# Attention and bilinear feed-forward on one core: probability sums by accumulating transfers in place of GpSimd and half of VectorE's additions

## The chip, the cores and the metric

The kernel runs on one core of a Trainium2 chip. The metric is the device time of one execution in microseconds (us), the median of several runs. The engines of the core are named as in the profile: PE is TensorE's matmul, PEld its weight loads, DVE is VectorE, ACT is ScalarE, POOL is GpSimd, SP is SyncE. L585 is line 585 of the kernel.

## What is computed

Attention in which a query sees only the keys whose nearest centroid is the same as its own, and then a bilinear feed-forward layer on its output:

```python
batch, n_heads, seq, head_dim = (4, 8, 768, 64); n_clusters = 16
q_assign = np.argmax(einsum('bhsd,hcd->bhsc', q_n, c_n), -1)   # same for k
mask = q_assign[:, :, :, None] == k_assign[:, :, None, :]
scores = scale * np.matmul(q, k.transpose(0, 1, 3, 2))
scores = np.where(mask, scores, -1000000000.0)
scores = scores - np.max(scores, axis=-1, keepdims=True)
attn = np.exp(scores)
attn = attn / (np.sum(attn, axis=-1, keepdims=True) + 1e-09)
attn_out = np.matmul(attn, v)
# bridge: x is (4 * 768, 512), then with d_ff = 1536
a = x @ w_a
b = x @ w_b
out = a * b @ w_out
```

## The kernel before

Two heads are worked on at a time, a head pair `p`; there are 4 per batch element (`HP = 4`) and 16 in all. A pair has two halves of 384 queries (`HB = 384`), and each half six key tiles of 128 keys (`j` = 0 to 5). One half and one key tile make a unit `u`. Scores are laid out with keys on the partitions, so the sum over the keys, which the softmax divides by, has to be taken across partitions. The kernel first adds the six tiles of exponentials into one tile `acc` and then multiplies a matrix of ones by it.

The scores of two units are made, then their exponentials. There are four buffers for the exponentials `pt`, two for `acc` and two for the scores:

```python
ptp = pool("ptp", 4)
accp = pool("accp", 2)
...
ps_s = pool("ps_s", 2, PS)
...
        def exp():
            for u, s in zip(us, tiles):
                pt = ptp.tile([P, 2, HB], FP32, name="pt")
                nc.scalar.activation(out=pt, in_=s[:, :, 0:HB], func=AF.Exp,
                                     scale=SCALE)                      # L563
                probs[u] = pt
```

The additions, one instruction for each of the two heads `a`. In batch element 0 (`p < HP`) all are on VectorE and the sixth tile is left to the matmul with ones; in the others GpSimd takes most:

```python
    def add_up(u):
        p, hf, j = where(u)
        if j == 0 or j == NJ - 1 and p < HP:
            return
        if j == 1:
            accs[p, hf] = accp.tile([P, 2, HB], FP32, name="acc")
        acc = accs[p, hf]
        for a in range(2):

            many = p >= HP and (a == 1 or j > 3)
            eng = nc.gpsimd if many else nc.vector
            eng.tensor_tensor(                                         # L585
                out=acc[:, a, :],
                in0=probs[u - 1][:, a, :] if j == 1 else acc[:, a, :],
                in1=probs[u][:, a, :], op=ALU.add)
```

The sum across partitions, and the division. `across`, `invert` and `back` run on VectorE (L639, L642, L646), `apply` on GpSimd (L653) with one exception:

```python
    def denominators(p, hf):
        ps = apart()
        acc = accs.pop((p, hf))
        terms = [acc]
        if p < HP:
            terms.insert(0, probs[p * UPP + hf * NJ + NJ - 1])
        for n, t in enumerate(terms):
            for a in range(2):
                nc.tensor.matmul(out=ps[a * D:(a + 1) * D, 0:HB], lhsT=ones,
                                 rhs=t[:, a, :], start=(n == 0),        # L619
                                 stop=(n == len(terms) - 1))
        ...
    def normalize(p, hf):
        ...
        def apply():
            eng = nc.vector if (p, hf) == (HP - 1, 0) else nc.gpsimd
            eng.tensor_tensor(out=x, in0=x, in1=den, op=ALU.mult)       # L653
```

The loop over groups of two units. Each engine works through its own instructions in the order in which they stand here:

```python
    for g in range(NG + 3):
        p, l = divmod(g, GPP)                  # GPP = 6 groups per head pair
        now = (2 * g, 2 * g + 1)
        before = (2 * g - 2, 2 * g - 1)
        ...
        if 0 < g < NG:
            score(now)                         # TensorE, then the exponentials
        check_inverses()
        if 0 < g <= NG:
            for u in before:
                add_up(u)
        flush_w()
        if 1 < g <= NG:
            weigh(before)                      # probabilities by v, TensorE
        late = int(g > EARLY)                  # EARLY = 25
        if g % 3 == late and 0 < g - late:
            ... denominators(...)              # of the half that ended
        if g < NG:
            ready[l]()
        ...                                    # pieces of the feed-forward layer
        # (TensorE; PSUM read by ScalarE and VectorE), steps of normalize, and
        # the rounding of weight parts, are spread over the rest of the group
```

The feed-forward layer of one batch element runs between the groups of the next. GpSimd also multiplies in it (`done`, L824), and adds in the rounding of the 36 parts of the weights (`round_w`, L295); VectorE waits for that addition in `flush_w` (L302).

Of the kernel before, what the change touches and what calls it, by code (L numbers as in the profile page):

```python
# [14 lines left out]
ALU = mybir.AluOpType  # L15
# [123 lines left out]
def short_path(nc, tc, ctx, c, cn, centroids_in, casts, n_far, q, k, v,  # L139
# [7 lines left out]
    HP = H // 2  # L147
# [387 lines left out]
    probs, accs, O_of, den_of, xTs = {}, {}, {}, {}, {}  # L535
# [5 lines left out]
    def where(u):  # L541
        p, l = divmod(u, UPP)
        hf, j = divmod(l, NJ)
        return p, hf, j
# [29 lines left out]
# [4 lines that stand above are left out]
        if j == 1:  # L578
            accs[p, hf] = accp.tile([P, 2, HB], FP32, name="acc")
        acc = accs[p, hf]  # L580
        for a in range(2):

            many = p >= HP and (a == 1 or j > 3)
            eng = nc.gpsimd if many else nc.vector
            eng.tensor_tensor(  # L585
                out=acc[:, a, :],
                in0=probs[u - 1][:, a, :] if j == 1 else acc[:, a, :],
                in1=probs[u][:, a, :], op=ALU.add)

    def weigh(us):  # L590
        for u in us:
# [497 lines left out]
    for g in range(NG + 3):  # L1089
        p, l = divmod(g, GPP)  # L1090
# [9 lines left out]
# [3 lines that stand above are left out]
# [300 lines left out]
```

## Time and profile before

| | |
|---|---|
| time, median of 3 runs | 1044.93 us (1044.05 to 1045.06) |
| span of the profiled run | 1042.1 us |
| granted TensorE clock | 0.998 |
| transfers, all queues | 46.49 MB, 120523 packets |
| additions of exponentials, VectorE | 136 of 128 x 384 |
| additions of exponentials, GpSimd | 168 of 128 x 384 |

Times of instructions are given as a sum in us and a mean in ns, with the shape of the output and the inputs. Behind the bar stands the idle time of the engine just before them and the instruction that ended most of it. Matmuls overlap in TensorE, so a group's busy time is shorter than count times mean.

### The profile page before, as it was taken

What the parts mean: (1) busy time and instruction counts of PE and PEld (TensorE: products, weight loads), DVE (VectorE), ACT (ScalarE), POOL (GpSimd) and SP (SyncE); (2) the same over time, 40 slices, a digit from 0 to 9 for tenths busy, and PEclk for the clock granted to TensorE, in tenths of its full rate; (3) what the DMA queues carried; (4) which work ended last, traced back from release to release, by engine and by line L of the source; (5) the groups of instructions that cost most, each with busy time, mean ns of one, the idle gap of its engine ahead of it and who ended that gap; (6) DMA issues with size and microseconds to landing.
All of it is one profiled execution on the core that took longest, in us unless ns stands there. A gap on an engine that the chain in (4) does not pass through costs nothing.

```text
span 1042.1 us, 17904 instructions
## 1 busy us (share of the span) xinstructions
PE 1030.8 (99%) x7158; PEld 500.5 (48%) x7158; DVE 658.7 (63%) x1314; ACT 302.8 (29%) x590; POOL 334.1 (32%) x310
## 2 busy tenths in 40 slices
PE   8999999999999999999999999999999999999997
PEld 5443444444445554444444555444444565444565
DVE  6777888889847447555546746755454835554652
ACT  5665333233322222332323122333232201111100
POOL 1111255555633332343443421444333310211100
PEclk9999999999999999999999999999999999999999
DMA  7334253525220121203020030300000000000001
GB/s 183 87 86 86 70 123 105 127 70 142 63 49 21 30 51 27 35 4 47 5 46 4 23 66 25 46 2 20 1 5 1 12 30 22 1 1 1 3 30 34
DMA packets 120523, 46.49 MB, mean 45 GB/s; under 512 B 106608, under 2 KB 115824, under 8 KB 120432
## 3 DMA queue, kind: packets, MB, share of 16 engines
q1 hardware_dynamic: 120016, 44.85, 18.7%
q8 instruction: 58, 0.95, 0.4%
q10 hardware_dynamic: 416, 0.43, 0.1%
q14 instruction: 33, 0.27, 0.1%
HBM read 37.78 MB, written 6.29 MB: 42 GB/s over the span
## 4 chain that ended last, share of the span: by engine, by line
PE 95%; DVE 2%; issue 1%; POOL 0%; DMA 0%; ACT 0%; DVEq 0%; POOLq 0%
PE m L679 63%; PE s L554 15%; PE O L596 13%; PE s L619 2%; PE m L619 1%; PE s L370 1%; PE m L370 0%; PE m L354 0%; DMA h<-in_q_dram 0%; DVE xT L910 0%; DVE raw L910 0%; PE m L430 0%; POOL xT L653 0%; PE m L384 0%; DVE h L919 0%
## 5 line engine op out<-in xcount | busy, mean ns | idle before, releaser
L563 ACT ACTIVATE pt<-s 128x768 f32<-128x768 f32 x192 | 145.3, 809 | 202.5 <-PE s L554 146.4
L585 POOL TENSOR_TENSOR acc<-acc,pt 128x384 f32<-128x384 f32 x144 | 155.6, 1100 | 60.0 <-ACT pt L563 45.9
L596 PE MATMUL O<-pt,v 128*64 128x384 f32 x768 | 145.1, 499 | 0.0
L554 PE MATMUL s<-qkT 64*128 64x384 f32 x768 | 139.7, 483 | 0.0
L824 POOL TENSOR_TENSOR h<-h,ha 128x384 f32<-128x384 f32 x54 | 56.1, 1041 | 255.6 <-DVE ha L818 255.1
L679 PE MATMUL m<-xT,wb_sb 128*64 128x384 f32 x672 | 116.4, 487 | 0.0
L679 PE MATMUL m<-xT,wa_sb 128*64 128x384 f32 x672 | 116.2, 487 | 0.2 <-DVE xT L653 0.2
L818 DVE TENSOR_TENSOR ha<-ha,m 128x384 f32<-128x384 f32 x72 | 39.6, 551 | 106.5 <-PE m L679 80.4
L815 ACT COPY h<-m 128x384 f32<-128x384 f32 x72 | 34.4, 478 | 184.9 <-PE m L679 184.9
L596 PEld LDWEIGHTS O<-pt,v 128*64 128x64 f32 x768 | 46.7, 136 | 85.7 <-issue 80.0
L679 PE MATMUL m<-wo_sb,h 128*64 128x256 f32 x768 | 86.7, 380 | 0.0
L554 PEld LDWEIGHTS s<-qkT 64*128 64x128 f32 x768 | 70.7, 187 | 31.2 <-issue 0.2
L818 DVE TENSOR_TENSOR h<-h,m 128x384 f32<-128x384 f32 x72 | 39.5, 549 | 72.3 <-PE m L679 46.9
L679 PE MATMUL m<-raw 128*64 128x384 f32 x432 | 78.9, 486 | 0.0
L653 POOL TENSOR_TENSOR xT<-xT,acc 128x384 f32<-128x384 f32 x31 | 32.5, 1048 | 143.2 <-DVE acc L646 143.0
L679 PEld LDWEIGHTS m<-xT,wb_sb 128*64 128x64 f32 x672 | 47.9, 137 | 61.2 <-issue 56.3
L679 PEld LDWEIGHTS m<-xT,wa_sb 128*64 128x64 f32 x672 | 48.0, 137 | 60.4 <-issue 55.6
L679 PEld LDWEIGHTS m<-wo_sb,h 128*64 128x64 f32 x768 | 55.0, 137 | 31.0 <-issue 5.0
L585 DVE TENSOR_TENSOR acc<-acc,pt 128x384 f32<-128x384 f32 x96 | 63.4, 687 | 2.3 <-ACT pt L563 1.0
L679 PE MATMUL m<-xT,h 128*64 128x256 f32 x576 | 64.5, 379 | 0.0
L679 PE MATMUL m<-xT,size 128*64 128x384 f32 x288 | 52.7, 487 | 0.0
L679 PEld LDWEIGHTS m<-xT,h 128*64 128x64 f32 x576 | 41.4, 137 | 22.3 <-issue 2.0
(168 smaller groups left out, 1312.3 us busy)
## 6 DMA issues: line engine op xcount, KB each, us to landing
raw<-in_moe_w_a_dram SPq DMA_DIRECT2D x12, 512.0 KB, 3.9
raw<-in_moe_w_b_dram SPq DMA_DIRECT2D x12, 512.0 KB, 3.6
raw<-in_moe_w_out_dram SPq DMA_DIRECT2D x12, 512.0 KB, 3.7
qk<-in_q_dram SPq DMA_DIRECT2D x48, 96.0 KB, 3.2
qk<-in_k_dram SPq DMA_DIRECT2D x48, 96.0 KB, 3.6
v<-in_v_dram SPq DMA_DIRECT2D x24, 192.0 KB, 3.8
out_dram<-rest SPq DMA_DIRECT2D x24, 128.0 KB, 1.7
v<-in_v_dram SPq DMA_DIRECT2D x4, 384.0 KB, 4.5
```

The costliest lines, as they stand in the source:

```text
L370: nc.tensor.matmul(out=ps[32 * kq:32 * kq + 32, 0:HB], lhsT=cTb[:, hp, :], rhs=qkTs[p][:, kq * HB:(kq + 1) * HB], start=True, stop=True)
L554: nc.tensor.matmul(out=s[:, a, 0:HB], lhsT=Ts[p][r, S + j * P:S + (j + 1) * P], rhs=Ts[p][r, hf * HB:(hf + 1) * HB], start=start, stop=not ...
L563: nc.scalar.activation(out=pt, in_=s[:, :, 0:HB], func=AF.Exp, scale=SCALE)
L585: eng.tensor_tensor(out=acc[:, a, :], in0=probs[u - 1][:, a, :] if j == 1 else acc[:, a, :], in1=probs[u][:, a, :], op=ALU.add)
L596: nc.tensor.matmul(out=O_of[0][a * D:(a + 1) * D, 0:HB], lhsT=vs[p][:, a, j, :], rhs=probs[u][:, a, :], start=(j == 0), stop=(j == NJ - 1))
L619: nc.tensor.matmul(out=ps[a * D:(a + 1) * D, 0:HB], lhsT=ones, rhs=t[:, a, :], start=(n == 0), stop=(n == len(terms) - 1))
L653: eng.tensor_tensor(out=x, in0=x, in1=den, op=ALU.mult)
L679: nc.tensor.matmul(out=ps[half], lhsT=lhsT[:, half], rhs=rhs, **kw)
L815: nc.scalar.copy(out=box[name], in_=box["X"][:, 0:HB])
L818: nc.vector.tensor_tensor(out=box[name], in0=box[name], in1=box[bank][:, 0:HB], op=ALU.add)
L824: nc.gpsimd.tensor_tensor(out=to, in0=to, in1=box[name], op=ALU.mult)
```

## The change

The sums of batch element 0 stay on VectorE, but both heads are added in one instruction of 768 columns. In batch elements 1 to 3, VectorE adds the first two key tiles of a half in one instruction, and each of the four others is added by a transfer, issued by GpSimd, that reads the tile of exponentials and adds it to `acc` where it lies. The aim is to take the additions off VectorE and GpSimd, and to have them done by the DMA engines.

```diff
@@ def add_up(u):
         if j == 1:
             accs[p, hf] = accp.tile([P, 2, HB], FP32, name="acc")
         acc = accs[p, hf]
-        for a in range(2):
-
-            many = p >= HP and (a == 1 or j > 3)
-            eng = nc.gpsimd if many else nc.vector
-            eng.tensor_tensor(
-                out=acc[:, a, :],
-                in0=probs[u - 1][:, a, :] if j == 1 else acc[:, a, :],
-                in1=probs[u][:, a, :], op=ALU.add)
+        if p < HP:
+            nc.vector.tensor_tensor(out=acc, in0=probs[u - 1] if j == 1 else acc,
+                                    in1=probs[u], op=ALU.add)
+            return
+        if j == 1:
+            nc.vector.tensor_tensor(out=acc, in0=probs[u - 1], in1=probs[u],
+                                    op=ALU.add)
+        else:
+            nc.gpsimd.dma_start(out=acc, in_=probs[u], accum_op=ALU.add)
```

In the changed kernel the lines behind this place are one further on: L619 becomes L620, L653 becomes L654.

## The prediction

> **What bounds the kernel now.** I read the engine table of the page first, then the stretches of the span, then who TensorE waited for, then GpSimd's groups, and last the timeline around the end of one half of a head pair.
>
> From the page and from the table of stretches (time, then busy time of PE, PEld, DVE, ACT, POOL with counts, granted clock, DMA share, GB/s):
>
> ```profile
> PE 1030.8 (99%) x7158; PEld 500.5 (48%) x7158; DVE 658.7 (63%) x1314; ACT 302.8 (29%) x590; POOL 334.1 (32%) x310
> ...
> 0.00:104.00 104.00, 99.78 (x672) 47.99 (x672) 79.07 (x164) 61.59 (x110) 18.04 (x22) 1.00 0.46 111
> 104.00:208.00 104.00, 103.26 (x646) 44.33 (x648) 90.88 (x139) 36.46 (x67) 48.21 (x39) 1.00 0.42 106
> 208.00:312.00 104.00, 104.00 (x664) 45.49 (x662) 81.21 (x123) 35.74 (x69) 55.63 (x46) 1.00 0.34 81
> 312.00:840.00 528.00, 527.67 (x3700) 256.62 (x3698) 307.25 (x641) 145.47 (x290) 189.75 (x182) 1.00 0.12 24
> 840.00:1042.00 202.00, 196.09 (x1484) 106.06 (x1478) 100.33 (x251) 23.55 (x54) 22.49 (x23) 0.99 0.05 14
> ```
>
> TensorE is the bound, with no slack. The probability sums of batch elements 1 to 3 are made from 104 to 840 us, 736 us in which PE is busy for all but 1.07 us (0.74 + 0 + 0.33). Its other idle time is 4.2 us before 104 us and 5.9 us behind 840 us; behind 840 us next to no sums are made. Removing work from DVE or POOL can therefore give back next to nothing. From the groups by shape and the list of waits:
>
> ```profile
> L585 POOL TENSOR_TENSOR acc<-acc,pt 128x384 f32<-128x384 f32 x144 | 155.6, 1100 | 60.0 <-ACT pt L563 45.9 <-DVE acc L585 11.5
> L585 POOL TENSOR_TENSOR acc<-pt 128x384 f32<-128x384 f32 x24 | 29.6, 1232 | 0.9
> L585 DVE TENSOR_TENSOR acc<-acc,pt 128x384 f32<-128x384 f32 x96 | 63.4, 687 | 2.3 <-ACT pt L563 1.0
> L585 DVE TENSOR_TENSOR acc<-pt 128x384 f32<-128x384 f32 x40 | 24.9, 638 | 14.9 <-POOL xT L653 10.3 <-ACT pt L563 4.6
> ...
> PE m L619 <- DVE acc L585: 2.1, 1, 2.1
> ```
>
> The 304 additions cost 273.5 us of two engines that are not the bound. One matmul in the whole run waited for a sum: 2.1 us, in batch element 0. So the question is only whether the new transfers are late for TensorE. From the timeline of GpSimd and ScalarE:
>
> ```profile
> 636.61 1.37 POOL L585 TENSOR_TENSOR acc<-pt 128x384 f32<-128x384 f32 x1
> 638.06 2.48 POOL L585 TENSOR_TENSOR acc<-acc,pt 128x384 f32<-128x384 f32 x2
> 654.30 1.00 POOL L653 TENSOR_TENSOR xT<-xT,acc 128x384 f32<-128x384 f32 x1 [13.76 <-DVE acc L646]
> 655.25 4.08 POOL L585 TENSOR_TENSOR acc<-acc,pt 128x384 f32<-128x384 f32 x4
> ...
> 665.55 1.51 ACT L563 ACTIVATE pt<-s 128x768 f32<-128x768 f32 x2 [0.68 <-PE s L554]
> ```
>
> The last two key tiles (four additions of one head each) are summed from 655.25 to 659.33 us; the matmuls with ones that read the sum start at 667.33 us, 8 us later. GpSimd reached these additions only at 655.3, because the multiplication of L653 stands ahead in its queue and waited for DVE.
>
> **What the Trainium skill says.** (1) "DMA: Bandwidth & Descriptors", section "Anatomy of one DMA — SWDGE (gpsimd) path": a transfer issued by GpSimd costs about 2.0 us plus its bytes at 436 GB/s. No such transfer is in this trace; the nearest, 12 KB from SBUF to SBUF issued by SyncE (ohT<-oh), lands in 1.8 us. (2) "Collectives: The Full Stack", section "The bandwidth ceiling: the fold count and why AG ≠ RS ≠ AR": an adding transfer runs at half the rate of a copy, because of two source reads and not because of the addition. No run here shows it yet. (3) "DMA: Bandwidth & Descriptors", section "Rules for kernel authors": an accumulating transfer must await the earlier one to the same bytes. The built program agrees: each of a half's second to fourth transfers waits for the completion of the one before. (4) "SBUF — State Buffer", section "Who interferes with whom": a DVE instruction with two SBUF inputs contends with GpSimd's reads. The trace agrees: the DVE additions have a median of 552 ns and a maximum of 1632.
>
> **The change, part by part.**
>
> *Removed.* GpSimd loses 168 additions: 155.6 + 29.6 = 185 us of its 334. All lie beside TensorE's work: 0 us on the path.
>
> *VectorE in one instruction.* Batch element 0 has 8 halves of 4 additions, before 64 instructions of 384 columns, now 32 of 768. DVE takes 550 ns for 384 columns and 414 for 256 (L818, L942), so 1.06 ns a column, and 768 should take about 0.96 us instead of 2 x 0.55. Elements 1 to 3 keep one addition of 768 per half (24 of them) where 72 of 384 were. DVE's 136 additions (63.4 + 24.9 = 88.3 us) become 56 of 0.96, or 54 us: DVE falls from 659 to some 625. Worth on the path: part of the one 2.1 us wait; I put down 1 us.
>
> *Added.* 24 halves x 4 key tiles = 96 transfers, each 128 x 768 x 4 B = 393 KB from SBUF to SBUF, issued by GpSimd in its queue, four in a row dependent on each other. Their latency L, from issue to landing, is the number that decides. By the skill's formula with twice the data: 2.0 + 2 x 0.90 = 3.8 us. By the trace: packets of 1024 B have a median of 48 ns and of 4096 B of 159 ns (packet records), so 0.036 ns a byte and about 122 ns for a row of 3072 B; 128 rows over 16 engines, read twice, are 8 x 2 x 122 = 1.95 us; with 1.8 us of fixed time (ohT<-oh) and about 1 us for GpSimd to write the descriptors (my estimate, from the skill's remark that this path's first byte takes about 1 us), 4.8 us. I take 4.8, and think 3.8 to 7 likely.
>
> *What TensorE tolerates.* In the half shown, the transfer of tile 5 (the fifth) goes out at 655.3, that of tile 6 at 655.3 + L, and lands at 655.3 + 2L. The matmuls at 667.3 allow L of up to 6.0; the exponentials of 665.55 and 666.26, which reuse the two buffers the transfers read, allow 10.2 and, by 2L = 10.96, 5.5. A group of two key tiles takes 8.3 to 12 us of TensorE (distances between the exponentials), so in other halves the limit is lower. I laid such a chain through all 24 halves: exponentials, matmuls and GpSimd's other instructions where the trace has them, GpSimd held 1 us by each issue, no feedback. The sum of how late the sums come to their matmuls:
>
> - L = 4.0: 1.5 us in 2 halves; 4.5: 4.5 us in 4; 5.0: 13 us in 8
> - L = 5.5: 26 us in 11; 6.0: 44 us in 14; 7.0: 105 us in 23
>
> At 4.8 that is about 9 us. GpSimd also stands still while a transfer waits for the one before, and with it the multiplications of L653 and L824 and, until 36 weight parts are rounded, L295, for which DVE waits in L302 and so drains PSUM later. From 24 halves I add some 3 us. Sum: 1044.9 - 1 + 9 + 3 = 1056 us.
>
> **Rivals.** *Hidden anyway*: if L is 4.2 or less, every sum is there in time and the kernel ends at 1043 to 1047. For it: the formula's 3.8, and DMA engines only 12% busy from 312 to 840 us. Against: the 512 KB weight loads need 3.6 to 3.9 us with one read, and from 104 to 312 us the DMA engines are already 34 to 42% busy. *The transfers become the bound*: four dependent ones per half against about 30 us of TensorE (736 / 24 = 30.7). At L = 6.5 the list gives over 60 us, near 1115; at 8 (4 x 8 = 32) the chain is as long as the half itself and the time goes past 1150. For it: the addition's rate is shown nowhere in this trace. *GpSimd's blocked queue* is the third: with short transfers still, delayed L295 or L653 hold DVE, PSUM banks fill, and some 10 to 20 us are lost in the first two stretches. Against: GpSimd loses 185 us of work, and TensorE has three PSUM banks in turn. *A gain of over 2%* would need 21 us of PE's 11.3 us idle time; it can't come from this change.
>
> **Range and chances.** The 2% limit, 1065.8 us, is crossed at L of about 5.3. I give L below 4.3 three chances in ten, 4.3 to 5.3 three, above it four. That gives faster 0.02, same 0.56, slower 0.42, and a range of 1043 to 1115 about 1056.
>
> **What would show it.** Right: POOL busy falls by at least 100 us, DVE to 610 to 635, transfers land in 4 to 5.5 us, and PE's new idle time stands before L619's matmuls with acc (now one line on) and is spread unevenly over the halves. Waits of the exponentials for DMA without idle PE would be tolerated lateness. Wrong: L below 4 with time lost all the same (then it is GpSimd's queue, seen as DVE waiting for POOL in L302 or L653), or L above 6, in which case PE idles in nearly every half and the estimate of the transfer is what failed.

## The result and the profile after

The changed kernel takes 1054.89 us (median of 4 runs, 1053.03 to 1056.17) against 1044.99 us: a ratio of 1.0094, 95% interval 1.0077 to 1.0111. It is 0.9% slower, within 2%.

From the page of the changed kernel, the engine table and the chain that ended last:

```profile
PE 1036.1 (98%) x7158; PEld 506.4 (48%) x7158; DVE 590.5 (56%) x1234; ACT 303.3 (29%) x590; POOL 237.2 (23%) x238
...
PE 85%; DMA 5%; DVE 4%; issue 3%; POOL 2%; ACT 0%; POOLq 0%; DVEq 0%; ACTq 0%
```

GpSimd is rid of 97 us and VectorE of 68 us, and neither shows in the time. The span grew from 1042.1 to 1054.4 us, 12.3 us, and PE's row splits them: 5.3 us more busy, and so 7.0 us more idle. (The profiled run is the longest of the four, and that of the kernel before, 1043.85 us, is shorter than all others of it; the medians differ by 9.9 us.) The same matmuls took longer. The stretches show the clock that was granted meanwhile (columns as before):

```profile
104.00:208.00 104.00, 100.18 (x608) 42.85 (x610) 75.61 (x124) 36.08 (x66) 31.47 (x28) 0.97 0.62 134
208.00:312.00 104.00, 101.87 (x632) 43.64 (x630) 66.02 (x112) 33.54 (x64) 37.84 (x35) 0.98 0.62 133
312.00:840.00 528.00, 527.45 (x3684) 255.32 (x3682) 268.82 (x605) 146.98 (x291) 126.14 (x131) 1.00 0.43 77
```

Most of the loss lies before 312 us, where the weights are still being rounded: PE idles 3.8 and 2.1 us there, and its granted clock is 0.97 and 0.98. From 312 to 840 us, with over two thirds of the transfers (70 of 96), PE idles 0.55 us, against 0.33 us before. One more wait, of 1.52 us, follows at 856.69 us. Whom TensorE waited for (us in total, times, longest):

```profile
PE s L620 <- DMA acc<-pt: 6.9, 5, 2.4
PE m L620 <- DVE acc L582: 2.4, 1, 2.4
```

From the page, the group of the transfers, and their size and median time to landing; below, from the answer on L589, the spread of that time:

```profile
L589 POOL DMA_DIRECT2D acc<-pt x96 | 83.0, 865 | 262.8 <-DMA acc<-pt 147.9
...
acc<-pt POOLq DMA_DIRECT2D x96, 384.0 KB, 4.1
...
DMA to landing us min/median/max: 3.9/4.1/7.0
```

A transfer lands 4.1 us after its issue in the median, but 20 of the 96 need more than 4.8 us. GpSimd stood still 147.9 us for a transfer before. The exponentials waited 13.9 us, 8 times, for transfers that still read their buffers; no matmul with scores waited on that account, so this lateness is tolerated, as the prediction allowed. The half that the prediction worked out by hand is tolerated, as it said: the timeline has the last two transfers 4.4 us apart, and the matmul with ones long after.

```profile
663.71 1.00 POOL L654 TENSOR_TENSOR xT<-xT,acc 128x384 f32<-128x384 f32 x1 [10.85 <-PE m L680]
664.66 0.87 POOL L589 DMA_DIRECT2D acc<-pt  x1
669.08 0.85 POOL L589 DMA_DIRECT2D acc<-pt  x1 [3.56 <-DMA acc<-pt]
...
676.75 0.81 PE L620 MATMUL s<-acc,ones 128*64 128x384 f32 x4
```

A half that is late, from the timelines of GpSimd, VectorE, ScalarE and TensorE in order of time:

```profile
176.96 0.86 POOL L589 DMA_DIRECT2D acc<-pt  x1 [4.73 <-DMA acc<-pt]
177.52 1.59 POOL L295 TENSOR_TENSOR wb_sb<-wb_sb,rest 128x512 f32<-128x512 f32 x1
...
179.14 0.69 DVE L302 SCALAR_TENSOR_TENSOR wb_sb<-size,wb_sb 128x512 f32<-128x512 f32 x1 [4.25 <-POOL wb_sb L295]
...
181.34 0.81 ACT L563 ACTIVATE pt<-s 128x768 f32<-128x768 f32 x1 [0.60 <-PE s L554]
...
182.16 1.28 POOL L295 TENSOR_TENSOR wa_sb<-wa_sb,rest 128x512 f32<-128x512 f32 x1 [3.06 <-DVE rest L290]
183.41 0.99 POOL L654 TENSOR_TENSOR xT<-xT,acc 128x384 f32<-128x384 f32 x1
184.35 1.02 POOL L589 DMA_DIRECT2D acc<-pt  x1
188.96 0.85 POOL L589 DMA_DIRECT2D acc<-pt  x1 [3.59 <-DMA acc<-pt]
...
194.06 0.87 PE L620 MATMUL s<-acc,ones 128*64 128x384 f32 x4 [2.36 <-DMA acc<-pt]
```

The two queues hold each other up. A transfer waited 4.73 us for the one before; behind it stood L295, and for L295 VectorE waited 4.25 us. So VectorE gave the next part to GpSimd late, and the addition of that part and L654 stood ahead of the half's last two transfers: the exponentials of the fifth key tile were ready at 182.15 us, and their transfer went out at 184.35, 2.2 us later. The last one landed when TensorE had waited 2.36 us. Right after, the table of stretches shows the clock (the third figure from the end):

```profile
195.00:198.00 3.00, 3.00 (x14) 0.83 (x14) 1.52 (x3) 1.68 (x4) 0.00 (x0) 0.50 1.50 148
```

PE is busy throughout, at half clock. The clock records have three such stretches of 3.41 us, from 106.06, 194.81 and 256.25 us, each right after a wait (2.37, 2.36 and 2.13 us). If each costs half its length, they cost 3 x 1.7 = 5.1 us (an estimate), close to PE's additional busy time of 5.3 us. A half, below, is numbered from 0 over the whole kernel, two to a head pair; half 9 is the late one shown.

### The profile page after: what moved, and what is told of

It reads as the page before. It is cut to its first block, busy times and chain, and to the rows that moved or that the text cites. A ratio compares the mean times of both kernels' runs of the same rounds, so it can differ in the third digit from the quotient of the medians.

```text
span 1054.4 us, 17804 instructions
## 1 busy us (share of the span) xinstructions
PE 1036.1 (98%) x7158; PEld 506.4 (48%) x7158; DVE 590.5 (56%) x1234; ACT 303.3 (29%) x590; POOL 237.2 (23%) x238
## 4 chain that ended last, share of the span: by engine, by line
PE 85%; DMA 5%; DVE 4%; issue 3%; POOL 2%; ACT 0%; POOLq 0%; DVEq 0%; ACTq 0%
PE m L680 56%; PE s L554 13%; PE O L597 11%; DMA acc<-pt 5%; PE s L620 2%; PE s L370 1%; PE m L620 1%; PE m L354 0%; POOL xT L654 0%; PE m L370 0%; DVE acc L582 0%; POOL wa_sb L295 0%; POOL acc L589 0%; DVE rest L290 0%; PE O L1058 0%
## 5 line engine op out<-in xcount | busy, mean ns | idle before, releaser
L589 POOL DMA_DIRECT2D acc<-pt x96 | 83.0, 865 | 262.8 <-DMA acc<-pt 147.9
L680 PE MATMUL m<-xT,wb_sb 128*64 128x384 f32 x672 | 118.4, 493 | 0.0
L680 PE MATMUL m<-xT,wa_sb 128*64 128x384 f32 x672 | 116.0, 486 | 0.0
L825 POOL TENSOR_TENSOR h<-h,ha 128x384 f32<-128x384 f32 x54 | 56.6, 1051 | 209.0 <-DVE ha L819 208.7
L680 PE MATMUL m<-wo_sb,h 128*64 128x256 f32 x768 | 86.8, 379 | 0.0
L680 PEld LDWEIGHTS m<-xT,wb_sb 128*64 128x64 f32 x672 | 49.0, 139 | 63.3 <-issue 57.3
L680 PE MATMUL m<-raw 128*64 128x384 f32 x432 | 78.9, 486 | 0.0
L680 PEld LDWEIGHTS m<-xT,wa_sb 128*64 128x64 f32 x672 | 48.5, 137 | 59.6 <-issue 54.8
L680 PEld LDWEIGHTS m<-wo_sb,h 128*64 128x64 f32 x768 | 56.1, 137 | 29.9 <-issue 5.0
L680 PE MATMUL m<-xT,h 128*64 128x256 f32 x576 | 64.6, 379 | 0.0
L654 POOL TENSOR_TENSOR xT<-xT,acc 128x384 f32<-128x384 f32 x31 | 33.7, 1087 | 116.9 <-DVE acc L647 67.2
L680 PE MATMUL m<-xT,size 128*64 128x384 f32 x288 | 52.7, 487 | 0.0
L680 PEld LDWEIGHTS m<-xT,h 128*64 128x64 f32 x576 | 42.1, 137 | 21.5 <-issue 2.1
L816 ACT COPY ha<-m 128x384 f32<-128x384 f32 x54 | 25.8, 478 | 90.3 <-PE m L680 86.8
```

The lines of the kernel that those rows point to most:

```text
L589: nc.gpsimd.dma_start(out=acc, in_=probs[u], accum_op=ALU.add)
L680: nc.tensor.matmul(out=ps[half], lhsT=lhsT[:, half], rhs=rhs, **kw)
L816: nc.scalar.copy(out=box[name], in_=box["X"][:, 0:HB])
L825: nc.gpsimd.tensor_tensor(out=to, in0=to, in1=box[name], op=ALU.mult)
```

## The experiments

Edits are to the changed kernel unless the text says otherwise. The kernel before had a median of 1044.19 us beside the first eight and 1044.53 us beside the last two; ratios are to it.

**Sums read one group later.**

```diff
-        late = int(g > EARLY)
+        late = 2 * int(g > EARLY + 1)
```

> The changed kernel, with the matmuls that read a sum put one group of two units later in TensorE's queue for batch elements 1 to 3 (about 10 us more time for the transfers). Theory 'late sums': the loss is TensorE waiting for the transfers before these matmuls (6.9 us) and the halved clock that follows two of the waits (2 x 1.7 us), so both vanish: about 1045 us, with at most the wait and the clock dip of batch element 0 left over (105 us). Rival 'blocked queue': GpSimd standing still between dependent transfers holds VectorE and through it TensorE; it is not touched, so the time stays above 1051. Rival 'traffic': 38 MB more of transfers slow the engines' reads or the other transfers; not touched either, stays at 1055.

1050.48 us, ratio 1.0054 (1.0040 to 1.0068): between the theories. No matmul waits for a sum's transfer any more, but TensorE's list of waits has a new head:

```profile
PE s L554 <- DMA ohT<-oh: 3.7, 3, 1.4
PE m L620 <- DVE acc L582: 2.4, 1, 2.4
PE s L620 <- ACT pt L563: 1.4, 1, 1.4
```

and in VectorE's timeline, ahead of the one-hot tile that was late at 239.56 us:

```profile
220.97 0.69 DVE L302 SCALAR_TENSOR_TENSOR wb_sb<-size,wb_sb 128x512 f32<-128x512 f32 x1 [5.95 <-POOL wb_sb L295]
```

So "late sums" alone is not enough. That the blocked queue costs as well is read from the order of time here (VectorE's waits in L302 for L295 are 37.6 us, against 25.7 in the changed kernel and 9.1 before); the next two runs test it.

**The rounding's addition on VectorE.** It takes GpSimd out of VectorE's way; the transfers stay.

```diff
-        nc.gpsimd.tensor_tensor(out=w, in0=w, in1=rest, op=ALU.add)
+        nc.vector.tensor_tensor(out=w, in0=w, in1=rest, op=ALU.add)
```

> The changed kernel with the addition in the rounding of the 36 weight parts (L295) on VectorE, so that VectorE no longer waits for GpSimd's queue there. With the sums one group later the time was 1050.5 and not 1045, and TensorE's waits left over stood before the one-hot tiles, which VectorE made late after waits of up to 6 us for L295 behind a transfer. Theory 'late sums and blocked queue, each about half': the waits for one-hot tiles can't arise and the sums of halves 8, 9 and 11 start earlier: 1047 to 1051. Theory 'late sums alone': about 1053 to 1055. Rival 'traffic': 1055.

1050.84 us, ratio 1.0064 (1.0046 to 1.0082). Halves 9 and 11 are no longer late; half 31 (1.52 us) and half 29 (0.30 us) still are. Half 8, which was expected to be earlier, waits 2.83 us instead of 0.37, with a dip: its last transfer, issued at 157.70 us, took 6.2 us to land. A weight load of 512 KB was issued at 157.84 us; that it is the reason is not shown.

**Both edits together.**

> Both: sums read one group later, and L295 on VectorE. Theory 'late sums and blocked queue': nothing of the loss is left but the wait and the dip at 105 us: 1043.5 to 1046. Rival 'traffic' (38 MB more on the DMA engines make one-hot tiles and loads land late, whatever the queues do): the waits before the one-hot tiles stay, 1049 to 1051.

1044.98 us, ratio 1.0004 (0.9995 to 1.0013): the loss is gone, with all 96 transfers still made and the DMA engines 66 and 64% busy in the two stretches. "Traffic" falls as a cause of its own. It isn't without effect: the one-hot transfers of 12 KB land in 2.6 us here and in 1.8 us before, and single transfers of sums need up to 8.8 us, but no matmul waits for either any more. The two edits were not tried on the kernel before; PE idles only 1.07 us there from 104 to 840 us, so they have next to nothing to gain in it. Of the waits in dispute, TensorE's list has only that of batch element 0 left:

```profile
PE m L620 <- DVE acc L582: 3.1, 1, 3.1
```

**The part for batch element 0 alone** (an edit to the kernel before), and **the transfers alone** (batch element 0 as before).

```diff
+        if p < HP:
+            nc.vector.tensor_tensor(out=acc, in0=probs[u - 1] if j == 1 else acc,
+                                    in1=probs[u], op=ALU.add)
+            return
         for a in range(2):
```

> The first kernel with only the part for batch element 0: one instruction for both heads; GpSimd and VectorE add for the others as before. The wait at 105 us was 2.10 us before and 2.37 after, and after it the clock halved for 3.4 us. Theory 'one instruction is later for the first head': the first matmul waits for 768 columns instead of 384, so 0.3 to 0.5 us are lost, and 1.7 us more if the dip belongs to it: 1045 to 1047.5. Rival 'VectorE saves': 1044 or less.

> The changed kernel with batch element 0 as it was (one instruction for each head); the transfers stay. Theory 'late sums': the four or five waits for transfers and two clock dips stay, the dip at 105 us goes if it belongs to the one instruction: 1052.5 to 1055. If the transfers were not the main part, 1048 or less.

The first takes 1044.65 us, ratio 0.9997 (0.9989 to 1.0006): no difference, and less than the 1045 to 1047.5 expected, though its profile has the 2.37 us wait with a dip. The second takes 1055.03 us, ratio 1.0100 (1.0085 to 1.0116): the transfers are the whole loss. Its wait at 105 us is 2.10 us, as in the kernel before, and yet a dip follows, which the profile of before has not. So the dip at 105 us doesn't belong to the one instruction. It seems to come and go in the kernel before, too: of its 33 runs beside the last two experiments, the 14 with a mean clock of 0.997 have a median of 1045.43 us, the other 19 of 1044.30 us.

**Idle time filled in two halves.**

```diff
+        if p * 2 + hf in (9, 11):
+            for _ in range(2):
+                for a in range(2):
+                    nc.tensor.matmul(out=ps[a * D:(a + 1) * D, 0:HB], lhsT=ones,
+                                     rhs=wa_sb[:, 0, 0:HB], start=True, stop=True)
```

> The changed kernel, with four matmuls of no use (about 1.5 us) ahead of the matmuls that read the sums of halves 9 and 11, the two halves whose waits of 2.36 and 2.13 us were each followed by 3.4 us at half clock. Theory 'idle halves the clock': the waits shrink to under 1 us, the two clock dips vanish, and the time falls by 2 x 1.7 = 3.4 us to about 1051.5, although TensorE has more to do. Rival 'clock by chance or by load': the dips stay, and the time is unchanged or up to 3 us longer.

The waits shrank to 0.47 and 1.68 us (under 1 us was expected of both), and both dips are absent from the clock records. The time, 1053.76 us, ratio 1.0093 (1.0080 to 1.0107), is not told apart from the changed kernel's 1.0094: the gain expected from this edit isn't shown by the times, and new waits of 0.18 and 0.91 us appeared at 297 and 312 us. The mean clock of the five runs is 0.995 to 0.999, against 0.994 to 0.996 of the changed kernel. So the profile supports that idle time brings the dips; what a dip costs in time is not shown by this run.

**One transfer per head.**

```diff
-            nc.gpsimd.dma_start(out=acc, in_=probs[u], accum_op=ALU.add)
+            for a in range(2):
+                nc.gpsimd.dma_start(out=acc[:, a, :], in_=probs[u][:, a, :],
+                                    accum_op=ALU.add)
```

> The changed kernel with each transfer cut into one for each head (192 of 196 KB); the two heads depend on different bytes, so head 1 is under way while head 0 lands. GpSimd issues twice as often (1.72 us per key tile instead of 0.86). If a transfer's time is mostly data (4.1 us for 393 KB, two reads), a head lands in about 3.1 us and a key tile takes about 3.5 to 4 us instead of 4.4: fewer late sums, 1049 to 1053. If it is mostly fixed time, the step grows to about 5 us, and the late sums with it: 1062 or more.

1050.38 us, ratio 1.0050 (1.0032 to 1.0068), as for a transfer that is partly data. From the list of transfers (count, size, median time to landing):

```profile
acc<-pt POOLq DMA_DIRECT2D x192, 192.0 KB, 3.5
```

and from TensorE's list of waits:

```profile
PE s L622 <- DMA acc<-pt: 2.1, 3, 1.3
```

Half the bytes land in 3.5 us instead of 4.1, and the two heads overlap. The waits for sums fall from 6.9 to 2.1 us.

**A fifth transfer per half** (`nought` is a tile of zeros).

```diff
+            if j == NJ - 1:
+                nc.gpsimd.dma_start(out=acc[:, 0, 0:32], in_=nought,
+                                    accum_op=ALU.add)
```

> The changed kernel with a fifth, small transfer per half (zeros, 128 x 32, added to the same tile after the fourth has landed), which changes no number and puts the sum off by an estimated 3 us. Theory 'late sums': by the chain laid through the trace of the first kernel with 4.4 us a step and 3 us more at the end, 13 of 24 halves are late by 27 us together instead of 4 by 4; with dips after the waits over 2 us the time becomes 1075 to 1095. If lateness of the sums were tolerated (only GpSimd's blocked queue costs), 24 x 1 us of more blocking gives at most 1060.

1104.24 us, ratio 1.0564 (1.0543 to 1.0585), past the upper end. The small transfer lands in 2.1 us. TensorE's list of waits:

```profile
PE s L625 <- DMA acc<-nought: 37.8, 14, 8.8
PE s L556 <- DMA ohT<-oh: 3.5, 3, 1.4
```

Fourteen late halves instead of 13 expected, 37.8 us instead of 27, and eight stretches at half clock before the tail (the clock records; 41 us, so about 20 us lost by the same estimate). VectorE's waits in L302 for L295 grew to 55.6 us here (23.0 + 19.9 + 12.7), from 25.7 in the changed kernel, and the two longest waits for sums, 7.1 and 8.8 us, lie in the part with the rounding. That fits a mutual delay of the two queues that adds to the lateness; no run takes it out of this version, so its share is argued, not shown.

**The wait at 105 us taken away**, in the combined version and in the kernel before: the sum of half 6 is read one group later.

```diff
+        if g == 22:
+            denominators(HP - 1, 0)
-        if g % 3 == late and 0 < g - late:
+        if g % 3 == late and 0 < g - late and g != 21:
```

> The version with nothing of the loss left (sums one group later, L295 on VectorE; 1044.98 us), and the sum of half 6, which TensorE awaited for 3.09 us at 105 us with a clock dip behind it, read one group later too. Theory 'waits of TensorE are all there is': 3.1 us of wait and 1.7 us of dip go, 1040 to 1042. Rival: VectorE is the bound in this stretch, and its work is only awaited elsewhere (first feed-forward pieces, one-hot tiles): 1043 to 1045.

> The first kernel with only the sum of half 6 read one group later: the wait of 2.10 us at 105 us and, in the runs that have it, the dip go: 1041.5 to 1043. If the transfers give the combined version anything beyond this, that one is faster than this one by more than 0.5 us; theory: it isn't, because VectorE and GpSimd are not the bound.

1043.29 us, ratio 0.9985 (0.9978 to 0.9991), and 1044.16 us, ratio 0.9996 (0.9988 to 1.0005). Neither reached what was expected: the wait is broken up (in the first into 0.43, 1.33 and 0.79 us, before scores whose buffers are late and before L680), so VectorE's work is awaited elsewhere, as the rival said. With no single long wait there is no dip either. The first beats both kernels, by 0.15% over the one before. It is also 0.9 us faster than the second, more than the 0.5 us that were set as the sign that the transfers bring something of their own. So the theory that they don't is not confirmed; what the 0.9 us come from was not found.

## Why the prediction was right

*TensorE is the bound, and work taken off the others gives nothing back.* Confirmed: 97 us off GpSimd and 68 off VectorE, and the version without late sums or blocked queue is level with the kernel before (1.0004).

*A transfer's latency.* 4.8 us was estimated, 4.1 measured in the median, 4.4 from one issue to the next of the chain. The formula of the Trainium skill, "DMA: Bandwidth & Descriptors", section "Anatomy of one DMA — SWDGE (gpsimd) path", with the bytes doubled, gave an estimate of 3.8. The packet records tell which term was too large: a row of 3072 bytes takes 265 ns, against 2 x 122 = 244 estimated, so eight rows are 2.1 us, and about 2.0 us are left for what the prediction put at 1.8 + 1. Adding does double a packet's time or more: 1536 bytes take 151 ns with one transfer per head, and 65 ns in the plain transfers of the kernel before. That a second read is the reason, no run separates.

*What TensorE tolerates.* The right kind of loss, in the right place: 6.9 of the 7.0 us of new idle time stand before L620 and wait for transfers, in 5 halves (8, 9, 11, 29 and 31). The size was met by luck. A landing time of 4.1 us is one at which the rival *hidden anyway* had every sum in time and the kernel at 1043 to 1047 us. At the measured step of 4.4 us the chain gives 4 us in 4 halves (the figure stands with the fifth transfer), and the prediction's sum becomes 1044.9 - 1 + 4 + 3 = 1051 us. The chain had one latency for all transfers, where 20 of 96 need more than 4.8 us, and no delay of GpSimd's queue; 4.8 us for all of them made up for that.

*GpSimd's blocked queue: 3 us.* The rounding's addition moved away gains 3 us of the 10, the later reading 4, both 9 (ratios 0.0030, 0.0040 and 0.0090, each uncertain by some 0.002). So its share was mis-sized: it is not a small addition, but about as large as what the later reading gains. The path was another one, too. The prediction had VectorE drain PSUM late; TensorE's list has no such wait in the changed kernel. The delay went from GpSimd's queue over L302 and L295 back to that queue and so to the sums, and, with the sums read later, to the one-hot tiles.

*One instruction for both heads: 1 us gained.* The one step that was wrong in sign. The wait at 105 us went from 2.10 to 2.37 us, since the first matmul with `acc` needs both heads' 768 columns now. In the time it is nothing (0.9997).

*The other signs.* GpSimd's busy time fell by 96.9 us, not by 100: 185 us of additions went and 83 us of issuing came, and the prediction's own 96 issues of 1 us would have left only 89. VectorE fell to 590.5 us, not to 610 to 635. Its additions are 63.9 us now (28.6 + 27.7 + 7.6) where 54 were estimated; the other 44 us are instructions that the change doesn't touch and that became shorter, as L302 did, from 34.8 to 27.0 us. The prediction had cited the contention of VectorE and GpSimd that fits this, and left it out of its sum. In columns VectorE still adds 56 x 768 where it added 136 x 384, about a fifth less, so the title's "half" is too much.

*What was missing:* the clock. About 5 of the 12.3 us can be put down to half-clock stretches after waits. That is an estimate: of the versions with one such stretch, PE's busy time is 1032.5 us with the sums read later, 1032.0 with the part for batch element 0 alone, but 1030.8 with both edits, as in the kernel before. That 1056 was met within 1.1 us is owed to luck: a latency put too high made up for a clock that was left out and for 1 us of gain that didn't come.

## What to carry to other kernels

When TensorE has no slack, as here, work moved off another engine is worth next to nothing in itself (97 and 68 us brought no gain); ask what the new carrier's latency is, how many of its steps depend on each other, and how much time lies between the last and its reader. A queue in order that waits for a transfer (GpSimd's, 147.9 us here) delays all that stands behind it, also what has nothing to do with the transfer; look for other engines that wait for those instructions. If such a chain can't be shortened, read its result one round later and take the unrelated work out of that queue: here each gave back part of the loss, and both together all of it.

## What the hardware showed

A short idle time of TensorE can cost more than its length: 2.36 us were followed by 3.41 us at half clock. All half-clock stretches begin at multiples of 3.413 us from each other within a run (106.06, 194.81, 256.25: 26 and 18 intervals). In ten traces, all 20 such intervals with 2.09 us or more of PE idle time were followed by one at half clock, and none of the 17 with 0.9 to 1.73 us; from 1.79 to 1.98 us it went either way. One interval with only 0.79 us, itself at half clock, was followed by another at half clock. This is counted from matmul records, and is a rule of these traces alone. The Trainium skill, "TensorE: Matmul & The Clock Gate", section "HAM oscillation — how this bites in real kernels", speaks of gaps over about 3.4 us; here about 2 us are enough if they lie in one interval. That is why the wait of 2.10 us is followed by a dip in one trace and not in the other: in the kernel before it is split between two intervals, 1.25 us in the first.
